# A tuned transformer block rewritten: Strassen in the Q, K and V projections, an accumulator begun from a PSUM copy, hand-mapped memory, and transposes by DMA

## The chip, the cores and the metric

One core of a Trainium2 chip. The metric is the device time of one execution in microseconds (us), median of several runs. The kernel before takes 828.0 us (four runs, 825.25 to 830.36). All comparisons are between runs of the fast state; one slow run occurred and is set apart below, and one run stands alone, so that its state is unknown (d_pin_again).

Names used here: PE is TensorE's matmul stream and PEld its weight loads, DVE is VectorE, ACT is ScalarE, POOL is GpSimd, SP is the engine whose queue issues the DMAs. L574 means line 574 of the kernel in question.

## The reference

One block: layer norm, linear attention with feature map phi, output projection, residual; then layer norm, a gated ReLU unit, down projection, residual. S = 2048 tokens, D = 1024, F = 3584, 32 heads of 32.

```python
def _A_ref(x, wqkv, wo):                      # cut
    q, k, v = qkv[0], qkv[1], qkv[2]
    phi = lambda t: jnp.where(t > 0, t + 1, jnp.exp(t)) + 1e-6
    pq, pk = phi(q), phi(k)
    kv = jnp.einsum("bhsd,bhse->bhde", pk, v)
    z = jnp.einsum("bhsd->bhd", pk)
    num = jnp.einsum("bhqd,bhde->bhqe", pq, kv)
    den = jnp.einsum("bhqd,bhd->bhq", pq, z)[..., None] + 1e-6
    o = num / den
    return (...)(o, 0, 2, 1, 3).reshape(B, S, D) @ wo

def _B_ref(x, W_gate, W_up, W_down):          # cut
    gate = jnp.einsum("bsd,df->bsf", x, W_gate)
    up = jnp.einsum("bsd,df->bsf", x, W_up)
    gate = gate * (lambda x, dt: x.astype(dt))(gate > 0, gate.dtype)
    return jnp.einsum("bsf,fd->bsd", gate * up, W_down)

h = x + _A_ref(_layernorm(x, axis=-1), A_wqkv, A_wo)
h2 = h + _B_ref(_layernorm(h, axis=-1), B_W_gate, B_W_up, B_W_down)
```

## The kernel before

One level of Strassen (seven products of half size instead of eight) is already used in gate/up and in the down projection, with the products ordered so that three accumulate in one PSUM bank. Q, K and V are plain products. All 384 transposes of 128x128 are TensorE matmuls against an identity, eight to a PSUM bank, copied out by ScalarE (half of the first tile's by VectorE). Memory comes from pools, so the down weights can be loaded only when the gate/up pools close.

The instruction order of each engine is fixed when the kernel is built: a scheduler places every instruction by when it believes it to be ready. An engine then runs its list in order.

```python
def kproj(t):                                   # plain products; V and Q likewise
    ...
        for kc in range(KC):
            nc.tensor.matmul(ps[:, :NW], lhsT=xnT[:, kc, t * P:(t + 1) * P],
                             rhs=wkv_sb[:, kc, j * NW:(j + 1) * NW], ...)
...
def oT():                                       # attention: transpose on TensorE
    pt = ps_tp()
    for c in range(KC):
        nc.tensor.transpose(pt[:, c, :], st["o"][:, c * P:(c + 1) * P], ident[:])
    st["oT"] = bwork.tile([P, KC, P], BF16, tag="oT", name="oT")
    nc.scalar.copy(out=st["oT"][:], in_=pt[:])
...
def part1():                                    # gate/up: C11 = M1 + M2
    st["A"] = A = ps2.tile([P, 2, SW], FP32, tag="d", name="A")
    prod(A, 1, True)
    m1 = snap(A, "m1")                          # ScalarE copies M1 to SBUF
    Dp = ps2.tile([P, 2, SW], FP32, tag="d", name="Dp")
    prod(Dp, 2, True)
    finish_sum(Dp, m1, 0)                       # VectorE adds
...
b = []                                          # down weights: after the pools close, for each half
for k, h in ((0, 0), (1, 0), (0, 1), (1, 1)):
    x = dpool.tile([P, FH, DW], BF16, tag="wd", bufs=5, name="wd")
    nc.sync.dma_start(out=x[:], in_=wd_v[:, k * FH:(k + 1) * FH, h * DW:(h + 1) * DW])
    b.append(x)
```

Of the kernel before, what the change touches and what calls it, by code (L numbers as in the profile page):

```python
# [29 lines left out]

@with_exitstack
def block_kernel(ctx: ExitStack, tc: tile.TileContext, x, wqkv, wo, wg, wu, wd, out, H: int):
# [7 lines left out]
    assert Dh == 32 and D % P == 0 and S % P == 0 and F % P == 0  # L40
    HPC = P // Dh
    ST = S // P
    KC = D // P
    FC = F // P
    TB = min(512, S)
    NTB = S // TB
    TPB = TB // P
    HB = min(256, TB)
    NHB = TB // HB
    NW = min(512, D)  # L50
    NKB = D // NW
    CPB = NW // P
    NDW = P + HPC
    GPB = 512 // NDW
    n_kv_banks = (KC + GPB - 1) // GPB
    assert TPB * H <= 512

    _load_act_set(nc)

    consts = ctx.enter_context(tc.tile_pool(name="consts", bufs=1))  # L60
    ident = consts.tile([P, P], BF16, name="ident")
    from concourse.masks import make_identity

    make_identity(nc, ident[:])
    mask = consts.tile([P, NDW], FP32, name="mask")
# [5 lines left out]
    psctx = ExitStack()  # L71
    pspool = psctx.enter_context(tc.tile_pool(name="ps", bufs=1, space=PSUM))
    _xy = [0]

    def ps_tp():
        return pspool.tile([P, KC, P], BF16, tag="tp", bufs=2, name="tp")

    def ps_x(nm="x"):
        return pspool.tile([P, 512], FP32, tag="x", bufs=2, name=nm)

    def ps_y(nm="y"):
        return pspool.tile([P, 512], FP32, tag="y", bufs=4, name=nm)

    def ps_xy(nm="xy"):
        _xy[0] += 1
        return ps_x(nm) if _xy[0] % 3 != 0 else ps_y(nm)

    pqctx = ExitStack()
    pq_pool = pqctx.enter_context(tc.tile_pool(name="pq", bufs=1, side="right"))
    pqT = pq_pool.tile([P, KC, S], BF16, name="pqT")  # L90
    kvz = pq_pool.tile([P, KC, NDW], BF16, name="kvz")
    wo_sb = pq_pool.tile([P, KC, D], BF16, name="wo_sb")

    def phi_from_psum(ps_ap, dst_ap, pool, width):
        e = pool.tile([P, width], FP32, tag="phi_e", name="phi_e")
        nc.scalar.activation(out=e[:], in_=ps_ap, func=ACT.Exp)  # L96
        e2 = pool.tile([P, width], FP32, tag="phi_e2", name="phi_e2")
        nc.vector.tensor_scalar(out=e2[:], in0=e[:], scalar1=1.0, scalar2=PHI_EPS,
                                op0=ALU.min, op1=ALU.add)
        nc.vector.scalar_tensor_tensor(out=dst_ap, in0=ps_ap, scalar=0.0, in1=e2[:],  # L100
                                       op0=ALU.max, op1=ALU.add)

    qctx = ExitStack()
    qpool = qctx.enter_context(tc.tile_pool(name="qpool", bufs=1))
    qwork = qctx.enter_context(tc.tile_pool(name="qwork", bufs=2))
    wq_sb = qpool.tile([P, KC, D], BF16, name="wq_sb")
    xnT = qpool.tile([P, KC, S], BF16, name="xnT")
    wqkv_v = wqkv.rearrange("(kc p) n -> p kc n", p=P)

    def q_proj(b, ps_fn):  # L110
        for c in range(KC):
            ps = ps_fn("qp")
            for kc in range(KC):
                nc.tensor.matmul(ps[:, :TB], lhsT=wq_sb[:, kc, c * P:(c + 1) * P],  # L114
                                 rhs=xnT[:, kc, b * TB:(b + 1) * TB],
                                 start=(kc == 0), stop=(kc == KC - 1))
            phi_from_psum(ps[:, :TB], pqT[:, c, b * TB:(b + 1) * TB], qwork, TB)

    NQA = min(2, NTB)

    with ExitStack() as actx:
        apool = actx.enter_context(tc.tile_pool(name="apool", bufs=1))
        xpool = actx.enter_context(tc.tile_pool(name="xpool", bufs=min(6, ST)))
        awork = actx.enter_context(tc.tile_pool(name="awork", bufs=2))
        asmall = actx.enter_context(tc.tile_pool(name="asmall", bufs=4))

        ps_mm = ps_xy
        wkv_sb = apool.tile([P, KC, 2 * D], BF16, name="wkv_sb")
        kv_ps = [ps_y("kv_ps") for _ in range(n_kv_banks)]

        x_tiles = {}

        def load_x(t):
            x_sb = xpool.tile([P, D], BF16, tag="x_sb", name="x_sb")
            nc.sync.dma_start(out=x_sb[:], in_=xf[t * P:(t + 1) * P, :])
            x_tiles[t] = x_sb

        load_x(0)
        nxt = 1
        for j in range(NKB):  # L140
            nc.sync.dma_start(out=wkv_sb[:, :, j * NW:(j + 1) * NW],
                              in_=wqkv_v[:, :, D + j * NW:D + (j + 1) * NW])
            if nxt < min(TPB, ST):
                load_x(nxt)
                nxt += 1
        while nxt < min(TPB, ST):
            load_x(nxt)
            nxt += 1
        for j in range(NKB, 2 * NKB):
            nc.sync.dma_start(out=wkv_sb[:, :, j * NW:(j + 1) * NW],  # L150
                              in_=wqkv_v[:, :, D + j * NW:D + (j + 1) * NW])
        while nxt < min(6, ST):
            load_x(nxt)
            nxt += 1
        for j in range(NKB):
            nc.sync.dma_start(out=wq_sb[:, :, j * NW:(j + 1) * NW], in_=wqkv_v[:, :, j * NW:(j + 1) * NW])
        nc.sync.dma_start(out=wo_sb[:], in_=wo.rearrange("(kc p) n -> p kc n", p=P))

        def ln_T(t):
            if t not in x_tiles:  # L160
                load_x(t)
            x_sb = x_tiles.pop(t)
            nsub = (D + 511) // 512
            fm = D // nsub
            stats = asmall.tile([P, nsub, nc.vector.BN_STATS_DIM], FP32, tag="stats", name="stats")
            for i in range(nsub):
                nc.vector.bn_stats(out=stats[:, i, :], in_=x_sb[:, i * fm:(i + 1) * fm])  # L167
            mv = asmall.tile([P, nc.vector.BN_AGGR_DIM], FP32, tag="mv", name="mv")
            nc.vector.bn_aggr(out=mv[:], in_=stats[:])
            lnv = asmall.tile([P, 1], FP32, tag="lnv", name="lnv")  # L170
            nc.scalar.activation(out=lnv[:], in_=mv[:, 1:2], func=ACT.Ln, bias=LN_EPS, scale=1.0)
            rstd = asmall.tile([P, 1], FP32, tag="rstd", name="rstd")
            nc.scalar.activation(out=rstd[:], in_=lnv[:], func=ACT.Exp, scale=-0.5)
            xn = awork.tile([P, D], BF16, tag="xn", name="xn")
            nc.vector.tensor_scalar(out=xn[:], in0=x_sb[:], scalar1=mv[:, 0:1], scalar2=rstd[:],  # L175
                                    op0=ALU.subtract, op1=ALU.mult)
            pt = ps_tp()
            for kc in range(KC):
                nc.tensor.transpose(pt[:, kc, :], xn[:, kc * P:(kc + 1) * P], ident[:])  # L179
                if t == 0 and KC >= 2 and kc == KC // 2 - 1:  # L180
                    nc.vector.tensor_copy(out=xnT[:, 0:KC // 2, t * P:(t + 1) * P], in_=pt[:, 0:KC // 2, :])
            if t == 0 and KC >= 2:
                nc.scalar.copy(out=xnT[:, KC // 2:KC, t * P:(t + 1) * P], in_=pt[:, KC // 2:KC, :])
            else:
                nc.scalar.copy(out=xnT[:, :, t * P:(t + 1) * P], in_=pt[:])

        def kproj(t):
            pk = awork.tile([P, D], BF16, tag="pk", bufs=TPB + 2, name="pk")
            for j in range(NKB):
                ps = ps_mm("kp")  # L190
                for kc in range(KC):
                    nc.tensor.matmul(ps[:, :NW], lhsT=xnT[:, kc, t * P:(t + 1) * P],  # L192
                                     rhs=wkv_sb[:, kc, j * NW:(j + 1) * NW],
                                     start=(kc == 0), stop=(kc == KC - 1))
                phi_from_psum(ps[:, :NW], pk[:, j * NW:(j + 1) * NW], awork, NW)
            return pk

        def vproj_kv(t, pk):
            v_sb = awork.tile([P, KC, NDW], BF16, tag="v_sb", name="v_sb")
            nc.gpsimd.memset(v_sb[:, :, P:NDW], 1.0)  # L200
            for jj in range(NKB):
                j = NKB + jj
                ps = ps_mm("vp")
                for kc in range(KC):
                    nc.tensor.matmul(ps[:, :NW], lhsT=xnT[:, kc, t * P:(t + 1) * P],  # L205
                                     rhs=wkv_sb[:, kc, j * NW:(j + 1) * NW],
                                     start=(kc == 0), stop=(kc == KC - 1))
# [10 lines left out]
        for g in range(NTB):  # L218
            pks = {}
            for tt in range(TPB):  # L220
                t = g * TPB + tt
                if t + 1 < ST:
                    ln_T(t + 1)
# [13 lines left out]
    for b in q_proj_rest:  # L237
        q_proj(b, ps_y)
# [383 lines left out]
```

## Time and profile before

| | before |
|---|---|
| time, median (range) | 828.0 us (825.25 to 830.36) |
| profiled span | 825.0 us |
| TensorE busy | 782.2 us, 95%, 4,016 matmuls |
| first projection matmul | 10.65 us |
| Q/K/V | to 196.5 us |
| attention and output projection | to 298.6 us |
| gate/up | to 641.6 us |
| wait for the down weights | 8.0 us |
| down projection | to the end |

Lines of the page of the kernel before: busy time per engine, the DMA engines' mean busy share in tenths over 40 slices, two matmul groups (after the bar: busy us, mean ns of one, then idle time before them and what ended it), and one group of DMA issues (size, median us to landing).

```profile
span 825.0 us, 10025 instructions
...
PE 782.2 (95%) x4016; PEld 369.1 (45%) x4016; DVE 506.7 (61%) x845; ACT 216.2 (26%) x337; POOL 3.6 (0%) x31
...
DMA  9700000530222200040401304040000983892001
...
L510 PE MATMUL accA<-wd,hh 128*128 128x512 f16 (+1 forms) x336 | 74.9, 385 | 8.0 <-DMA wd<-in_B_W_down_dram 8.0
L315 PE MATMUL attn<-wo_sb,oT 128*128 128x512 bf16 x256 | 61.2, 387 | 10.8 <-ACT oT L304 10.7
...
wd<-in_B_W_down_dram SPq DMA_DIRECT2D x8, 1792.0 KB, 9.7
```

Read it so: TensorE is busy 95% of the span, so it bounds the kernel; the hole is in the L510 line, 8.0 us in which TensorE sat idle until the down weights (wd) landed. The L315 line shows 10.7 us of waits for transposed attention tiles. In back-to-back stretches 56 matmuls of 128x512 take 12.09 us, 0.216 us each; the mean of about 380 ns that the page gives is the time from the start of one pipelined matmul to its end, which overlaps with the next, and not what it costs. The DMA digits of the attention stage (the tenth to the fifteenth of the 40) are 0 to 2: the DMA engines are nearly idle there.

Two windows of the attention stage of the kernel before; columns are stretch, length, then busy us and number of instructions per engine, the granted clock, the DMA engines' busy share and GB/s.

```profile
core 0: us, PE busy (x) PEld busy (x) DVE busy (x) ACT busy (x) POOL busy (x), PEclk, DMA share, GB/s
...
215.00:235.00 20.00, 18.03 (x137) 10.20 (x136) 18.87 (x52) 7.22 (x18) 0.00 (x0) 1.00 0.29 93
235.00:255.00 20.00, 17.37 (x149) 10.52 (x148) 18.73 (x56) 8.55 (x20) 0.00 (x0) 1.00 0.29 97
```

VectorE (third group, 18.87 and 18.73 of 20 us) is full here, TensorE is not.

### The profile page before, as it was taken

To read this page: it belongs to the slowest core of one execution; us is meant where nothing else is said; L and a number is where in the kernel's file an instruction comes from. 1 tells how busy PE (TensorE), PEld (TensorE's weight loads), DVE (VectorE), ACT (ScalarE), POOL (GpSimd) and SP (SyncE) were. 2 spreads that over 40 slices of the span, in tenths; PEclk is the share of its full clock that TensorE was granted. 3 is DMA by queue.
4 is the path that set the end of the run, shared out by engine and by line. 5 is a ranking of instruction groups with operands and counts; after the bars stand their busy time and mean duration, and the time that the engine had idled before them with its cause. 6 is when DMAs were issued, how large, how long until landed. Compare 5 with 4: busy or idle time off the path is not lost.

```text
span 825.0 us, 10025 instructions
## 1 busy us (share of the span) xinstructions
PE 782.2 (95%) x4016; PEld 369.1 (45%) x4016; DVE 506.7 (61%) x845; ACT 216.2 (26%) x337; POOL 3.6 (0%) x31
## 2 busy tenths in 40 slices
PE   5999999998897979999999999999999699999998
PEld 3445554443454534444444444444444244444443
DVE  5756314386999965567657556765754784329832
ACT  3435434332334333322323332333332000000000
POOL 0000000000000000000000000000000000000000
PEclk9999999999999989999999999999999899999999
DMA  9700000530222200040401304040000983892001
GB/s 323 250 14 26 1 1 1 152 92 0 97 83 79 89 25 14 20 127 27 122 26 56 84 20 128 25 122 27 20 19 20 300 267 120 273 340 97 26 33 45
DMA packets 75678, 74.04 MB, mean 90 GB/s; under 512 B 3440, under 2 KB 67952, under 8 KB 75120
## 3 DMA queue, kind: packets, MB, share of 16 engines
q1 hardware_dynamic: 75632, 73.41, 27.9%
q8 instruction: 31, 0.51, 0.3%
q14 instruction: 15, 0.12, 0.1%
HBM read 57.67 MB, written 15.73 MB: 89 GB/s over the span
## 4 chain that ended last, share of the span: by engine, by line
PE 59%; DVE 2%; DMA 2%; issue 1%; ACT 0%; SPq 0%; ACTq 0%
PE A L396 24%; PE E L396 12%; PE accA L510 10%; PE Dp L396 6%; PE accE L510 6%; PE accD L510 1%; DMA wd<-in_B_W_down_dram 1%; DMA hres<-h_dram_1898 1%; DVE s_6330 L534 0%; DVE hh L536 0%; DVE o L522 0%; DVE wd L548 0%; DVE s_6331 L535 0%; ACT u_5732 L410 0%; DVE hh_5749 L447 0%
## 5 line engine op out<-in xcount | busy, mean ns | idle before, releaser
L510 PEld LDWEIGHTS <-hh 128*128 128x128 bf16 (+1 forms) x560 | 55.1, 99 | 75.5 <-issue 10.6
L510 PE MATMUL accA<-wd,hh 128*128 128x512 f16 (+1 forms) x336 | 74.9, 385 | 8.0 <-DMA wd<-in_B_W_down_dram 8.0
L315 PE MATMUL attn<-wo_sb,oT 128*128 128x512 bf16 x256 | 61.2, 387 | 10.8 <-ACT oT L304 10.7
L396 PEld LDWEIGHTS <-tg 128*128 128x128 f16 x448 | 43.8, 98 | 54.2 <-issue 1.4
L396 PEld LDWEIGHTS <-tu 128*128 128x128 f16 x448 | 43.8, 98 | 52.9
L205 PE MATMUL vp<-wkv_sb,xnT 128*128 128x512 bf16 x256 | 59.8, 379 | 0.0
L192 PE MATMUL kp<-wkv_sb,xnT 128*128 128x512 bf16 x256 | 59.6, 388 | 0.0
L114 PE MATMUL qp<-xnT,wq_sb 128*128 128x512 bf16 x256 | 56.2, 379 | 1.3 <-DVE pqT L100 1.3
L396 PEld LDWEIGHTS <-wg 128*128 128x128 bf16 x336 | 33.2, 99 | 41.6 <-issue 2.9
L396 PEld LDWEIGHTS <-wu 128*128 128x128 bf16 x336 | 33.2, 99 | 40.9 <-issue 2.2
L315 PEld LDWEIGHTS <-oT 128*128 128x128 bf16 x256 | 23.6, 99 | 38.2 <-ACT oT L304 13.6
L114 PEld LDWEIGHTS <-wq_sb 128*128 128x128 bf16 x256 | 24.9, 98 | 30.9 <-issue 1.9
L192 PEld LDWEIGHTS <-xnT 128*128 128x128 bf16 x256 | 25.0, 100 | 28.0 <-issue 2.2
L205 PEld LDWEIGHTS <-xnT 128*128 128x128 bf16 x256 | 24.0, 97 | 24.6
L445 ACT ACTIVATE rg<-A 128x512 bf16<-128x512 f32 x28 | 16.7, 597 | 68.1 <-PE A L396 68.1
L304 ACT COPY oT<-tp 128x1024 bf16<-128x1024 bf16 x16 | 16.2, 1012 | 55.9 <-PE tp L302 55.9
L417 DVE SCALAR_TENSOR_TENSOR hh<-gu 128x512 bf16<-128x512 bf16 x42 | 29.0, 690 | 1.0
L96 ACT ACTIVATE phi_e<-qp 128x512 f32<-128x512 f32 x32 | 19.1, 597 | 39.1 <-PE qp L114 37.8
L175 DVE TENSOR_SCALAR xn<-x_sb,mv,rstd 128x1024 bf16<-128x1024 bf16 x16 | 8.7, 544 | 33.4 <-PE tp L179 31.1
L208 ACT CAST v_sb<-vp 128x512 bf16<-128x512 f32 x32 | 18.7, 585 | 39.8 <-PE vp L205 39.6
L167 DVE BATCH_NORM_STATS2 stats<-x_sb 128x6 f32<-128x512 bf16 x32 | 20.4, 671 | 9.8 <-DMA x_sb<-in_A_x_dram 9.8
L96 ACT ACTIVATE phi_e<-kp 128x512 f32<-128x512 f32 x32 | 19.1, 596 | 27.0 <-PE kp L192 27.0
(589 smaller groups left out, 1250.4 us busy)
## 6 DMA issues: line engine op xcount, KB each, us to landing
wd<-in_B_W_down_dram SPq DMA_DIRECT2D x8, 1792.0 KB, 9.7
wg<-in_B_W_gate_dram SPq DMA_DIRECT2D x14, 512.0 KB, 5.0
wu<-in_B_W_up_dram SPq DMA_DIRECT2D x14, 512.0 KB, 6.7
x_sb<-in_A_x_dram SPq DMA_DIRECT2D x16, 256.0 KB, 7.8
wkv_sb<-in_A_wqkv_dram SPq DMA_DIRECT2D x4, 1024.0 KB, 8.9
x_res<-in_A_x_dram SPq DMA_DIRECT2D x16, 256.0 KB, 2.8
out_dram<-o SPq DMA_DIRECT2D x32, 128.0 KB, 1.8
wq_sb<-in_A_wqkv_dram SPq DMA_DIRECT2D x2, 1024.0 KB, 11.0
```

The lines of the kernel that those rows point to most:

```text
L96: nc.scalar.activation(out=e[:], in_=ps_ap, func=ACT.Exp)
L114: nc.tensor.matmul(ps[:, :TB], lhsT=wq_sb[:, kc, c * P:(c + 1) * P], rhs=xnT[:, kc, b * TB:(b + 1) * TB], start=(kc == 0), stop=(kc == KC ...
L167: nc.vector.bn_stats(out=stats[:, i, :], in_=x_sb[:, i * fm:(i + 1) * fm])
L192: nc.tensor.matmul(ps[:, :NW], lhsT=xnT[:, kc, t * P:(t + 1) * P], rhs=wkv_sb[:, kc, j * NW:(j + 1) * NW], start=(kc == 0), stop=(kc == KC ...
L205: nc.tensor.matmul(ps[:, :NW], lhsT=xnT[:, kc, t * P:(t + 1) * P], rhs=wkv_sb[:, kc, j * NW:(j + 1) * NW], start=(kc == 0), stop=(kc == KC ...
L208: nc.scalar.copy(out=v_sb[:, jj * CPB:(jj + 1) * CPB, 0:P], in_=ps[:, :NW].rearrange("p (c e) -> p c e", e=P))
L304: nc.scalar.copy(out=st["oT"][:], in_=pt[:])
L315: nc.tensor.matmul(ps[:, :NW], lhsT=st["oT"][:, c, :], rhs=wo_sb[:, c, j * NW:(j + 1) * NW], start=(c == 0), stop=(c == KC - 1))
L396: nc.tensor.matmul(ps[:, x, :], lhsT=w[x][m - 1][:, kc, :], rhs=left[m - 1][:, kc, :], start=(start and kc == 0), stop=(kc == KH - 1), ski ...
L417: nc.vector.scalar_tensor_tensor(out=d, in0=gu[:, 0, :], scalar=0.0, in1=gu[:, 1, :], op0=ALU.max, op1=ALU.mult)
L445: nc.scalar.activation(out=rg[:], in_=A[:, 0, :], func=ACT.Relu)
L510: nc.tensor.matmul(acc[:], lhsT=lhs[:, f, tt * P:(tt + 1) * P], rhs=rhs[:, f, :], start=(start and f == 0), stop=(f == FH - 1), skip_group ...
```

## The change

Intent: fewer TensorE matmuls (Strassen in Q, K and V; transposes moved to DMA), less VectorE work in the attention stage, one VectorE addition less per gate/up quad (the second accumulator starts as a PSUM-to-PSUM copy of the first product), and memory laid out by hand so that the down weights can be loaded early. It is a rewrite; this is its core, with cuts.

```diff
+# one Strassen quad; A, D, E are PSUM banks
+    def p2(self):
+        D = self.ring()
+        self.fork(D, self.A)          # ScalarE copies M1, PSUM to PSUM
+        self.prod(D, 2, False)        # M2 accumulates on it
+        self.c11(D)
 ...
-            ps = ps_mm("kp")
-            for kc in range(KC):
-                nc.tensor.matmul(ps[:, :NW], lhsT=xnT[:, kc, t * P:(t + 1) * P], ...)
+        def prod(ps, m, start):       # K, V: pair p is the tiles p and p + 8
+            for kc in range(KH):
+                nc.tensor.matmul(ps, lhsT=left[m - 1][:, kc, :], rhs=right[m - 1][:, kc, :], ...)
 ...
-            for kc in range(KC):
-                nc.tensor.transpose(pt[:, kc, :], xn[:, kc * P:(kc + 1) * P], ident[:])
+            for k in range(2):
+                nc.sync.dma_start_transpose(out=XH[i][k][:, :, r:r + P], in_=xn[:, k * 512:(k + 1) * 512])
 ...
-            pt = ps_tp()
-            for c in range(KC):
-                nc.tensor.transpose(pt[:, c, :], st["o"][:, c * P:(c + 1) * P], ident[:])
+            nc.sync.dma_start_transpose(out=self.oT, in_=o)
 ...
+    for p in range(NP):               # K and V
+        pk, kq = k_quad(p)
+        qs.run(kq)
+        if p + 1 < NP:
+            ln_pair(p + 1)            # layer norm, normalisation on GpSimd, transpose by DMA
+        v, vq = v_quad(p)
+        qs.run(vq)
+        if p + 1 < NP:
+            x_sums(p + 1, 1)          # VectorE: Strassen operand sums of the next pair
 ...
+    hh1_ring = ring_of([at(132 + i, [SW]) for i in range(8)])     # spilled gate/up results
 ...
-            x = dpool.tile([P, FH, DW], BF16, tag="wd", bufs=5, name="wd")
+    wdb = [at(a, [FH, DW]) for a in (180, 128, 142, 156)]         # b11, b21, b12, b22; KB addresses
+    for x_, (k, h) in zip(wdb, ((0, 0), (1, 0), (0, 1), (1, 1))):
+        nc.sync.dma_start(out=x_, in_=wd_v[:, k * FH:(k + 1) * FH, h * DW:(h + 1) * DW])
```

## The prediction

> **What bounds the kernel now.** TensorE. The page gives it 95% busy of an 825 us span; VectorE 61%, ScalarE 26%. In the back-to-back stretches of the timeline 56 matmuls of 128x512 take 12.09 us, so one costs 0.216 us. By the windows and the timeline: first projection matmul at 10.7 us; Q/K/V to 196.5 us, TensorE full; attention and output projection 196.5 to 298.6 us; gate/up to 641.6 (28 quads of 12.09 = 338.5 of 343 us); 7.9 us in which TensorE waits for the down weights (the waits view: 8.0 us); down projection 175.5 us, of which 784 matmuls are 169.3. Only the attention stage is not TensorE-bound: VectorE is busy about 90% there, one 128-row tile every 5.65 us, about 107 us of VectorE work for 16 tiles, while TensorE's own work is about 78 us (256 large matmuls 55 us, 128 small and 256 transposes at about 0.06 us).
>
> **What the change does.**
> 1. Strassen in Q, K, V only (the output projection stays plain): 768 large matmuls become 672, 96 x 0.216 = -20.7 us.
> 2. 352 of the 384 TensorE transposes go to DMA: -21 us of TensorE work, all of it critical in the Q/K/V stage (-6), the rest in attention.
> 3. Attention VectorE work falls: BN_STATS (2 x 0.69), reciprocals and adds (1.07) and the 0.54 normalisation leave VectorE for ScalarE and GpSimd. By my sum 6.7 falls to about 3.9 us a tile, 62 us, below TensorE's 63. The second half of Q and the first gate/up products are interleaved there. I expect 78 us instead of 102, about 15 of them waits.
> 4. The down weights' memory is hand-mapped: the first block is loaded before gate/up ends (-8), and the weight combinations are not built twice for the second half (20 us of VectorE, mostly off the path; the stage falls by 2 to 3).
> 5. Added: PSUM-to-PSUM copies on ScalarE (1.01 us for 128x1024, as the snapshots). In gate/up the copy goes to a bank that the previous quad's last product leaves: its multiply (0.69) and the copy (1.01) must fit behind 9 matmuls (1.94 us). With about 0.1 us hand-overs that is even or 0.1 to 0.2 us short per quad: +3 to 6 us, offset by little.
> 6. Start: the first seven products need all four weight blocks and their VectorE sums (1.22 us each), for K and again for V. About 16 us of idle before steady state instead of 10.7: +5.
>
> DMA transposes of 128x1024 have no duration in this trace. The Trainium skill, "DMA: Bandwidth & Descriptors", Latency and other measured facts, gives 261 GB/s for DMA transpose; 256 KB is then an estimated 1 us, plus about 2 us as this trace's small transfers take. Two steps of lag (about 8 us) cover that.
>
> **Sum.** 16 + 161 (Q/K/V: 672 x 0.216 + 10 small + 6 waits) + 78 + 344 + 173 = 772; against a profile 3 us below the median.
>
> **Predicted: 770 us, 80% range 746 to 808. Faster by over 2%: 0.90, within 2%: 0.06, slower: 0.04.**
>
> **What would show it.** Page: TensorE near 96% busy; about 3,584 matmuls; VectorE under 460 us busy. Windows: gate/up 340 to 348 us; no 8 us hole before the down projection. Waits: TensorE waiting for the PSUM copy, under 0.3 us each. DMA issues: transposes landing in 2 to 4 us.
>
> **What would make it wrong.** Transposes that cost several us of DMA or queue time each: two per tile, in order on one queue with all loads; every engine runs a fixed order, so a late one stalls VectorE and then all. GpSimd normalisations over about 3 us, same result. The copy waiting for the whole product rather than half: 0.7 us per quad, +20 us.

## The result

| | before | after |
|---|---|---|
| time, median (range) | 828.0 us (825.25 to 830.36, 4 runs) | 791.55 us (788.05 to 793.07, 4 runs) |
| profiled span | 825.0 us | 790.3 us |
| TensorE busy | 782.2 us | 750.6 us, 3,583 matmuls |
| VectorE busy | 506.7 us | 459.2 us |

The ratio after to before is 0.9555 (95% interval 0.9525 to 0.9584). Ratios here are the mean time of one kernel's fast runs over the mean of the other's fast runs of the same rounds, so they are not quite the ratios of the medians that stand beside them.

The change is faster by 4.5%, about 22 us short of the point that was predicted. The page of the kernel after:

```profile
span 790.3 us, 9417 instructions
...
PE 750.6 (95%) x3583; PEld 341.0 (43%) x3583; DVE 459.2 (58%) x744; ACT 255.7 (32%) x481; POOL 41.2 (5%) x58
...
DMA  9355100318797833204022140310311920561011
...
L574 PE MATMUL psum<-mem 128*128 128x512 f16 (+1 forms) x1568 | 343.3, 379 | 1.2 <-ACT psum L270 1.1
...
L676 PE MATMUL psum<-mem 128*128 128x512 f16 (+1 forms) x784 | 172.1, 383 | 7.5 <-DVE mem L700 7.5
...
L321 PE MATMUL psum<-mem 128*128 128x512 f16 (+1 forms) x448 | 107.2, 394 | 13.6 <-DVE mem L343 5.0
```

TensorE is still 95% busy, with less to do. Gate/up (L574) waits 1.1 us in all for the PSUM copies (L270). The down group (L676) still has a hole, 7.5 us, but it now waits for VectorE (L700) and no longer for a DMA. The K/V group (L321) has 13.6 us of waits where the groups of K and V of before had none. And the DMA digits of the attention stage (tenth to fourteenth) are 7 to 9.

The same two windows of the attention stage, kernel after:

```profile
215.00:235.00 20.00, 16.88 (x84) 7.85 (x85) 16.41 (x44) 8.95 (x33) 3.62 (x3) 0.91 0.93 210
235.00:255.00 20.00, 18.27 (x106) 8.94 (x104) 12.34 (x32) 9.39 (x37) 6.16 (x4) 1.00 0.82 178
```

VectorE has room now (12.34 of 20 us in the second), but the DMA engines' share has gone from 0.29 to 0.93 and 0.82.

To see where TensorE's time goes I counted the matmuls of each stretch and took 0.2159 us for a large one and 0.062 us for a small one; what is left of the stretch is called lost. This is an estimate, good to about 1 us a row. It is given only for profiles with complete matmul records (as many matmuls as weight loads). The kernel after also runs 15 warm-up matmuls before its first product; they are not counted as work. Half clock counts as lost time, too. The last two columns are experiments that come below.

| lost TensorE time, us | before | after | operand sums pinned | one transpose per tile |
|---|---|---|---|---|
| start to 12 (before: to 10.65) | 9.4 | 10.8 | 10.4 | 10.1 |
| 12 to 100 | 2.4 | 18.9 | 11.4 | 8.2 |
| 100 to 200 | 4.7 | 1.7 | 2.7 | 2.4 |
| 200 to 300 | 20.9 | 16.0 | 14.0 | 15.9 |
| 300 to 608 (before: to 640) | 3.2 | 2.1 | | |
| from there to the end | 13.8 | 13.5 | | |

The sums: before loses 54.4 us and after 63.0, so TensorE's work fell by about 43 us (825.0 - 54.4 against 790.3 - 63.0). That is what 96 large matmuls (20.7 us) and 352 transposes (21.8 us at 0.062) come to. The expected saving of work is all there; 8.6 us of it net were given back as lost time: the Q/K/V stage (12 to 200 us) lost 13.5 us more than before, the attention stage 4.9 less. Some of the row from 12 to 100 is no wait: the granted clock was 0.50 from 12 to 16 us and 0.80 from 16 to 20 in this profile of the kernel after, 0.66 and 1.00 with operand sums pinned, and full with one transpose per tile. From 20 to 100 us alone the lost time is 14.9, 8.7 and 6.1 us in the three.

**The down hole.** TensorE's timeline of the kernel after around 608 us (start, length, group, in brackets the idle time just before it and what ended it):

```profile
start us, us, engine line op out<-in xcount [idle before <-releaser]
...
608.44 11.17 PE L676 MATMUL psum<-mem 128*128 128x512 bf16 x51
627.08 5.17 PE L676 MATMUL psum<-mem 128*128 128x512 f16 x12 [7.46 <-DVE mem L700]
```

Product 1 of the down projection (with five matmuls before 608) ends at 619.6. Then nothing for 7.46 us, and then 12 matmuls in 5.17 us, 0.43 us each, twice the usual. The built kernel, printed with a line of its own for each product, shows that six matmuls of product 6 stand ahead of product 2 in TensorE's list. Product 6 needs a chain of twelve VectorE subtractions of 2.02 us; product 2 needs a single weight block, b21. The queue that issues the loads, in the same stretch:

```profile
611.00 0.38 SPq L641 DMA_DIRECT2D mem<-in_B_W_down_dram  x1
613.50 0.32 SPq L582 DMA_DIRECT2D hh_dram<-mem  x1
613.91 5.71 SPq L641 DMA_DIRECT2D mem<-in_B_W_down_dram  x2
```

The first line is the load of b12; then the last spilled gate/up result (128 KB); then, in the third group, b22 at 613.9 and b21 only at 619.24. The view of waits of that queue:

```profile
engine line waited for: us in total, times, longest us
...
SPq L641 <- DMA hh_dram<-mem: 4.7, 1, 4.7
```

The issue of b21 waited 4.7 us for the spill to land, because the hand-made map gives b21 memory that the last spilled results still occupy.

**The Q/K/V stage.** VectorE's timeline of the kernel after near 95 us, then the TensorE group that was held:

```profile
start us, us, engine line op out<-in xcount [idle before <-releaser]
...
89.51 1.23 DVE L287 SCALAR_TENSOR_TENSOR mem<-mem 128x1024 bf16<-128x1024 f32 x1
94.48 0.43 DVE L248 TENSOR_TENSOR mem<-mem 128x512 f16<-128x512 bf16 x1 [3.75 <-DMA mem<-mem]
94.82 0.68 DVE L343 TENSOR_TENSOR mem<-psum,mem 128x512 bf16<-128x512 f32 x1
```

```profile
95.56 10.48 PE L321 MATMUL psum<-mem 128*128 128x512 bf16 x40 [2.00 <-DVE mem L343]
```

L248 is the first operand sum of the next pair; it waits 3.75 us for a transpose by DMA. Behind it in VectorE's list stands L343, an addition of the V result whose inputs were ready (the ScalarE copy that it needs ended at 91.18), and which frees the PSUM bank that TensorE needs. TensorE waits 2.00 us for it. This is how an engine with a fixed order passes one late transfer on to all. Some such waits were also followed by a lower clock:

```profile
core 0: us, PE busy (x) PEld busy (x) DVE busy (x) ACT busy (x) POOL busy (x), PEclk, DMA share, GB/s
44.00:48.00 4.00, 2.22 (x10) 0.74 (x8) 3.58 (x6) 1.26 (x3) 0.77 (x1) 1.00 0.74 162
48.00:52.00 4.00, 3.84 (x10) 1.39 (x11) 2.17 (x6) 0.58 (x1) 0.00 (x0) 0.57 0.60 152
...
626.00:630.00 4.00, 2.92 (x7) 0.99 (x8) 4.00 (x3) 0.00 (x0) 0.00 (x0) 0.50 1.11 379
```

The column before the DMA share is the granted clock. After the wait of 1.69 us that ended at 46.89 it was 0.57 from 48 to 52, and 0.50 from 626 to 630 after the wait of 7.46 us. The Trainium skill, "TensorE: Matmul & The Clock Gate", What's actually happening, states that the array drops to half rate after an idle window of about 3.4 us and needs as long a busy stretch to come back. The way back took 5.17 us here after the hole, somewhat more than one such window. That the clock fell after a wait of 1.69 us goes further than the page, but the length of a wait alone does not decide it: after waits of 1.34 us (ended at 64.62) and 1.65 us (at 70.74) it stayed full, and so it did in the trace of d_hh (below), whose Q/K/V stage is the same, after waits of 2.14 us (ended at 54.75) and 1.94 us (at 96.51). What decides stays open. So the same waits cost clock in one execution and none in another, and a part of each difference of a few us below can be this.

### The profile page after: what moved, and what is told of

Read it like the earlier page. It is cut to its first block, busy times and chain, and to the rows that moved or that the text cites. A ratio compares the mean times of both kernels' runs of the same rounds, so it can differ in the third digit from the quotient of the medians.

```text
span 790.3 us, 9417 instructions
## 1 busy us (share of the span) xinstructions
PE 750.6 (95%) x3583; PEld 341.0 (43%) x3583; DVE 459.2 (58%) x744; ACT 255.7 (32%) x481; POOL 41.2 (5%) x58
## 4 chain that ended last, share of the span: by engine, by line
PE 80%; DVE 6%; issue 5%; DMA 4%; ACT 2%; POOL 2%; SPq 1%; DVEq 0%; POOLq 0%; ACTq 0%
PE psum L574 41%; PE psum L676 20%; PE psum L321 7%; PE psum L418 6%; PE psum L482 4%; DMA mem<-mem 2%; DVE mem L700 2%; DMA mem<-in_A_wqkv_dram 1%; PE psum L458 1%; DVE mem L484 1%; POOL mem L240 1%; POOL mem L497 1%; DMA mem<-in_B_W_gate_dram 1%; ACT mem L274 1%; ACT mem L492 0%
## 5 line engine op out<-in xcount | busy, mean ns | idle before, releaser
L574 PE MATMUL psum<-mem 128*128 128x512 f16 (+1 forms) x1568 | 343.3, 379 | 1.2 <-ACT psum L270 1.1
L574 PEld LDWEIGHTS <-mem 128*128 128x128 f16 (+1 forms) x1568 | 152.8, 98 | 186.9 <-issue 7.6
L676 PE MATMUL psum<-mem 128*128 128x512 f16 (+1 forms) x784 | 172.1, 383 | 7.5 <-DVE mem L700 7.5
L602 DVE TENSOR_TENSOR mem<-psum,mem 128x1024 bf16<-128x1024 f32 x56 | 68.5, 1224 | 115.3 <-ACT mem L586 92.1
L676 PEld LDWEIGHTS <-mem 128*128 128x128 f16 (+1 forms) x784 | 77.1, 99 | 102.1 <-DVE mem L700 8.0
L321 PE MATMUL psum<-mem 128*128 128x512 f16 (+1 forms) x448 | 107.2, 394 | 13.6 <-DVE mem L343 5.0
L586 ACT COPY mem<-psum 128x1024 f32<-128x1024 f32 x56 | 56.7, 1012 | 111.8 <-PE psum L574 111.7
L321 PEld LDWEIGHTS <-mem 128*128 128x128 f16 (+1 forms) x448 | 44.5, 101 | 69.9 <-issue 19.8
L482 PE MATMUL psum<-mem 128*128 128x512 bf16 x256 | 60.1, 387 | 5.7 <-DMA mem<-mem 5.3
L592 ACT ACTIVATE mem<-psum 128x512 bf16<-128x512 f32 x56 | 33.4, 597 | 75.4 <-PE psum L574 75.4
L270 ACT COPY psum<-psum 128x1024 f32<-128x1024 f32 (+1 forms) x52 | 41.7, 803 | 37.1 <-DVE mem L594 29.8
L418 PE MATMUL psum<-mem 128*128 128x512 f16 (+1 forms) x224 | 52.6, 378 | 0.0
L700 DVE TENSOR_TENSOR mem<-mem 128x3584 f16<-128x3584 bf16 (+1 forms) x24 | 47.3, 2018 | 4.5 <-DMA mem<-hh_dram 2.7
L594 DVE TENSOR_TENSOR mem<-psum,mem 128x512 bf16<-128x512 f32 x56 | 38.7, 691 | 16.5 <-PE psum L574 12.6
L688 DVE TENSOR_TENSOR mem<-psum,mem 128x512 bf16<-128x512 f32 x32 | 22.1, 690 | 42.9 <-PE psum L676 42.7
L604 DVE SCALAR_TENSOR_TENSOR mem<-mem 128x512 bf16<-128x512 bf16 x56 | 38.7, 691 | 1.9
L418 PEld LDWEIGHTS <-mem 128*128 128x128 f16 (+1 forms) x224 | 21.2, 97 | 23.8 <-issue 2.2
```

The lines of the kernel that those rows point to most:

```text
L270: nc.scalar.copy(out=dst, in_=src)
L321: nc.tensor.matmul(ps, lhsT=left[m - 1][:, kc, :], rhs=right[m - 1][:, kc, :], start=(start and kc == 0), stop=(kc == KH - 1), skip_group_ ...
L418: nc.tensor.matmul(ps, lhsT=right[m - 1][:, kc, c * P:(c + 1) * P], rhs=left[m - 1][:, kc, :], start=(start and kc == 0), stop=(kc == KH - ...
L482: nc.tensor.matmul(ps, lhsT=self.oT[:, c, :], rhs=wo_sb[:, c, js], start=(c == 0), stop=(c == KC - 1))
L574: nc.tensor.matmul(ps[:, y, :], lhsT=w[y][m - 1][:, kc, :], rhs=left[m - 1][:, kc, :], start=(start and kc == 0), stop=(kc == KH - 1), ski ...
L586: nc.scalar.copy(out=u, in_=src)
```

## The experiments

My theory after reading the traces: (1) the down hole is a matter of order; (2) the Q/K/V waits come from late transposes together with VectorE's fixed order; (3) the PSUM copy costs nothing; (4) the transposes by DMA pay in the attention stage in spite of the load that they put on the DMA engines. Rivals: the data of product 2 are late themselves; VectorE simply has too much to do; the waits come from Strassen's sums and so cancel what Strassen saves in K and V.

| run | edit to the kernel after | median us | ratio to before |
|---|---|---|---|
| after | none | 791.55 | 0.9555 |
| d_pin | product 2 before product 6 | 795.05 | 0.960 (0.9577 to 0.9623) |
| d_pin_again | the same, one look | 792.1 | |
| d_hh | last spills off b21's memory | 780.05 | 0.9428 (0.9407 to 0.9449) |
| s_pin | operand sums behind V's addition | 783.63 | 0.9475 (0.9454 to 0.9497) |
| one_T | one transpose per tile in Q/K/V | 783.43 | 0.9464 (0.9442 to 0.9486) |
| kv_plain | K and V without Strassen | 794.23 | 0.9595 (0.957 to 0.9619) |
| gu_snap | no PSUM copy in gate/up | 792.58 | 0.9578 (0.9557 to 0.9599) |
| attn_peT | attention transposes on TensorE | 850.12 | 1.0272 (1.0243 to 1.0301) |
| att_peT2 | the same, a step later | 816.61 | 0.9867 (0.9838 to 0.9896) |
| att_lb | more lag and banks in attention | 789.64 | 0.9541 (0.952 to 0.9562) |
| best1 | s_pin + one_T + d_hh | 773.35 | 0.9347 (0.9322 to 0.9372) |
| best2 | best1 + two more | 771.0 | 0.9322 (0.9302 to 0.9341) |

All gave the right result. The runs came in rounds in which the kernel before had medians of 827.54, 826.92 and 827.04 us, against 828.0 in that of the kernel after. The ratios compare within a round, and by them the gains are somewhat smaller than by the medians, about 10.5 us for d_hh, 6.6 for s_pin and 7.5 for one_T. The intervals of d_pin, kv_plain, gu_snap and att_lb overlap with that of the kernel after, and that of best2 with that of best1: these differences are not clear of noise.

### d_pin and d_pin_again: product 2 first

```diff
-                nc.tensor.matmul(acc, lhsT=chunk(lhs, f)..., rhs=rhs[:, f, :], ...)
+                mm = nc.tensor.matmul(acc, lhsT=chunk(lhs, f)..., rhs=rhs[:, f, :], ...)
+                if pin and f == 0: tc.keep_in_program_order(mm)   # behind what was written before it
...
-            prod(A[tt], tt, sB, wd2, False)
+            prod(A[tt], tt, sB, wd2, False, pin=(s == 0))
```

> One edit to the changed kernel: in the first half of the down projection the first matmul of product 6 is pinned behind product 2 in TensorE's order (in the changed kernel six matmuls of product 6 stand ahead of product 2 and wait for VectorE's twelve subtractions until 627.1). Theory A (order): the hole of 7.5 us at 619.6 falls to under 1.5 us and the clock dip after it (about 2.6 us) goes with it, so 8 to 10 us come off 791.6: 781 to 784, ratio to before 0.943 to 0.947. Rival B (data): product 2's weights b21, whose load was issued at 611, are themselves late, so the hole only changes its owner to a DMA and the time stays within 2 us of 791.6. Rival C (VectorE): product 6 catches up with the subtractions later anyway, and the hole moves behind product 2: product 2 lasts 12.1 us, 619.6 to 631.7, longer than the 7.5 us that are missing, so no hole should appear there; if one does, it is under 1 us.

Measured: 795.05 us, no gain. Theory A failed. The first of its runs took 1122 us at a granted clock of 0.654 from end to end; it is not used for times. As the profile had fallen into that run, the kernel was run once more:

> The pinned kernel once more, for a profile in the fast state (the first profile of it fell in a slow run, clock 0.65). If b21's load, issued last at about 619 and landing about 10 us later, is what holds product 2 when product 2 goes first, the trace shows a wait of product 2 for a DMA of the down weights of 8.5 to 11 us ending at 628 to 631 in place of the 7.5 us wait for VectorE, and the time is 792 to 796. If instead there is no such wait, the reason for the pin's failure stays open.

Its TensorE timeline:

```profile
605.41 11.17 PE L676 MATMUL psum<-mem 128*128 128x512 bf16 x50
626.84 23.37 PE L676 MATMUL psum<-mem 128*128 128x512 bf16 x94 [10.26 <-DMA mem<-in_B_W_down_dram]
```

Product 2 now stands first and waits 10.26 us for a load of the down weights, in place of the 7.46 us for VectorE. The wait ended 1.2 us before the interval that I gave; its length and the time (792.1 us) were within theirs. Rival B was right: b21 is late itself. My text for d_pin had the cause of that wrong, though, for it took the load issued at 611 for b21; printing the four loads separately showed that b21 is issued last.

### d_hh: the memory that b21 waits for

```diff
+    hh1_last = ring_of([at(196 + i, [SW]) for i in range(8)])
...
-            return hh0(q, fc) if s == 0 else hh1_ring()
+            return hh0(q, fc) if s == 0 else (hh1_ring() if fc < FH - 2 else hh1_last())
```

> Reason for it: the pinned run was no faster, and its trace (slow state) shows product 2 waiting for a load of the down weights. The order of the queue in the changed kernel is b11 (560), b12 (611.0), b22 (613.9), and b21, which product 2 needs, last (619.24), because b21 shares memory with the last spilled gate/up results, and the last spill was issued at 613.5, behind the 1.8 MB of b12. One edit to the changed kernel: the results of the last two column blocks are put into 8 KB that are already free, so b21's memory is free earlier; the scheduler then issues b21 before the last spills and puts product 2 ahead of product 6 by itself (the build shows both). Theory A (memory reuse, then queue order, made the hole): the wait of 7.5 us and the half clock after it go, no new wait over 1 us in the down stage: 8 to 10 us less, 781 to 784, ratio 0.942 to 0.947. Rival B (VectorE's twelve subtractions until 627 limit whatever the order): product 6 waits instead, 789 to 792.

Measured: 780.05 us, 11.5 us less than the kernel after, slightly beyond the interval of theory A. The queue's timeline and TensorE's:

```profile
596.01 0.38 SPq L641 DMA_DIRECT2D mem<-in_B_W_down_dram  x1
...
608.80 0.38 SPq L641 DMA_DIRECT2D mem<-in_B_W_down_dram  x1
...
611.72 0.48 SPq L641 DMA_DIRECT2D mem<-in_B_W_down_dram  x1
```

```profile
606.24 34.05 PE L676 MATMUL psum<-mem 128*128 128x512 bf16 x155
```

b21 is issued at 596.0, before b12 (608.8) and b22 (611.7). From 606.24 on TensorE runs without a break (155 matmuls in 34 us in this cut of the timeline), and the view of waits shows none in the whole down stage. So the hole came from memory reuse: one 128 KB store in front of a load. (The hole and the half clock after it come to about 10 us. The rest is within the noise; in this profile the clock was also full after the waits of the Q/K/V stage, which the edit does not touch.) The store itself took 5.7 us to land against a median of 1.7 us for its kind, as it had been issued behind the 1.8 MB of b12. The Trainium skill, "DMA: Bandwidth & Descriptors", Queues, rings and completion order, says that on each DMA engine descriptors are consumed in ring order; this trace agrees with it. TensorE's odd order was the scheduler's answer to b21's late load: once the load is early, it puts product 2 first by itself.

### s_pin and one_T: the Q/K/V stage

s_pin changes VectorE's order and nothing else:

```diff
-        nc.vector.tensor_tensor(out=s1, in0=a21, in1=a22, op=ALU.add)
+        pin(nc.vector.tensor_tensor(out=s1, in0=a21, in1=a22, op=ALU.add))   # keep_in_program_order for pairs after the first
```

> One edit to the changed kernel: the first operand sum of each next pair in the Q/K/V stage (it waits for a transpose by DMA) is pinned behind the V addition traced before it on VectorE; no work is added or taken away. Theory A (VectorE's fixed order): the waits of K/V products for the V addition (1.69 us at 46.9, 1.34 at 64.6, 2.00 at 95.6) and the half clock after them go; lost TensorE time between 20 and 100 us falls from about 17 us to 6 to 10 us, total 782 to 787, ratio 0.945 to 0.951. Rival B (the transposes come too late anyhow): the wait moves to the next product, which needs the operand sums: K/V products wait for the sums instead, total within 2 us of 791.6. Rival C: amount of VectorE work in these 80 us, which the pin does not change: also within 2 us, with VectorE over 90% busy there.

Measured: 783.63 us. The place in VectorE's timeline that answers to the one shown above:

```profile
87.20 0.69 DVE L343 TENSOR_TENSOR mem<-psum,mem 128x512 bf16<-128x512 f32 x1 [0.48 <-ACT mem L274]
87.81 0.41 DVE L248 TENSOR_TENSOR mem<-mem 128x512 f16<-128x512 bf16 x1
```

L343 now runs first and L248 finds its transpose landed. Lost time from 12 to 100 us fell from 18.9 to 11.4 us. Not all of theory A came: the first of the three waits that it named is still there (1.65 us for L343, ended at 45.02), and the clock stayed full after it.

one_T leaves VectorE's order as it is and makes the transposes cheaper for the queue:

```diff
-            for k in range(2):
-                nc.sync.dma_start_transpose(out=XH[i][k][:, :, r:r + P], in_=xn[:, k * 512:(k + 1) * 512])
+            nc.sync.dma_start_transpose(out=at(16 * i, [KC, HS])[:, :, r:r + P], in_=xn)
```

> One edit to the changed kernel: in the Q/K/V stage each tile is transposed by one DMA of 128x1024 instead of two of 128x512. Theory A (the queue's issue time limits): issue time of the queue per tile falls from 3.2 us to about 1.9 us, the transposes land 1 to 4 us earlier, and waits at 70.7 and 95.6 that end with a transpose shrink: 786 to 790. Rival B (VectorE's order and the late statistics decide): the transposes wait for the normalised tile on GpSimd, not for the queue; total within 1.5 us of 791.6. If the issue time is in proportion to the columns and not per instruction, it stays 3.2 us a tile, which would also show here.

Measured: 783.43 us, better than theory A expected. The transposes of the Q/K/V stage, kernel after (24) and one_T (12): issue time in ns (min/median/max), first and last start, and time to landing.

```profile
L243 SPq DMA_TRANSPOSE mem<-mem x24: 1191/1244/1787, 38.7 to 91.9; - x24
...
DMA to landing us min/median/max: 2.4/2.5/3.7
```

```profile
L242 SPq DMA_TRANSPOSE mem<-mem x12: 1231/1232/2689, 36.3 to 81.6; - x12
...
DMA to landing us min/median/max: 3.0/3.2/4.0
```

The issue takes 1.24 us for 512 columns and 1.23 us for 1024: for these two widths it is a cost per instruction. In the kernel after GpSimd had the second tile of the pair ready at 89.05 us, but the last of the four transposes of the pair was issued at 91.9, behind the three others, and the sum that waited for it began at 94.48. With two per tile the second half lands about 1.24 + 2.5 us after the first issue begins, with one it is 3.2 us for all, and the queue is free for the next load 1.2 us earlier for each tile. What VectorE waited for transposes at L248 between 20 and 110 us, kernel after and one_T:

```profile
DVE mem L248 <- DMA mem<-mem: 7.1, 3, 3.7
```

```profile
DVE mem L248 <- DMA mem<-mem: 1.7, 2, 1.5
```

In s_pin this wait is absent. The order of L248, L343 and L295 in VectorE's list is the same in one_T as in the kernel after, so the same 7 us of waiting went in two ways: by transposes that come in time in the old order, or by an order in which nothing stands behind a late transpose. Neither the amount of VectorE work (rival C; both runs have the same within 1 us) nor the latency alone was the limit. The table of lost time puts 7.5 and 10.7 us into 12 to 100 us, of which 6.2 and 8.8 us lie between 20 and 100; the rest lies before 20 us, where the clock differs.

### kv_plain: what Strassen in K and V is worth

```diff
-        pk, kq = k_quad(p)
-        qs.run(kq)
+        pk = k_plain(p)          # four plain sums of 8 matmuls instead of seven products of 4
...
-        v, vq = v_quad(p)
-        qs.run(vq)
-        if p + 1 < NP:
-            x_sums(p + 1, 1)
+        v = v_plain(p)
+        x_sums(p, 1)             # now needed for Q alone
```

> One part of the change undone: K and V without Strassen (64 matmuls of 0.2159 us per pair and product instead of 56, 128 more in all... counted for K and V over 8 pairs: 64 against 56 for the two together, so 64 more, 13.8 us of TensorE work); operand sums are then needed for Q alone and nothing waits for them in this stage. Theory A (in the changed kernel the waits of this stage, 14.9 us between 20 and 100, ate the whole saving): those waits fall under 4 us, time 789 to 794. Rival B (the waits come from the transposes by DMA whatever the product): waits stay over 8 us, time 800 to 806.

Measured: 794.23 us, 2.7 us more than the kernel after, for 13.8 us more work. Neither theory holds whole. The waits did not go: they come to about 8 us between 38 and 75 us in its timeline (theory A said under 4). But the time is below rival B's interval. A part of the difference can be located: its start loses about 4 us less in the profile, as no product waits for sums of the weights and as the clock was full from 12 to 20 us in this profile (0.50 and 0.80 in that of the kernel after). VectorE's and TensorE's timelines show the same pattern as before:

```profile
72.11 0.43 DVE L248 TENSOR_TENSOR mem<-mem 128x512 f16<-128x512 bf16 x1 [6.18 <-DMA mem<-mem]
```

```profile
74.44 5.34 PE L352 MATMUL psum<-mem 128*128 128x512 bf16 x24 [2.27 <-DVE mem L363]
```

VectorE stands 6.18 us at L248 for a transpose, though no K or V product needs that sum any more, and TensorE waits 2.27 us for the K result (L363) queued behind it. So these waits come from a late transpose and the order, and not from a sum that a K or V product needs (the instruction that stands is still a Strassen sum, that of Q). It does not show that Strassen's sums cost nothing: about 11 us of the added work did not appear in the time, and only the start was located. In the kernel as it was changed, Strassen in K and V was worth about 3 us of its 13.8, which the noise does not tell from nothing. What it is worth once the waits are gone (in best1) was not run.

### gu_snap: the PSUM copy

```diff
-        self.fork(D, self.A)
-        self.prod(D, 2, False)
-        self.c11(D)
+        u1 = self.snap(self.A, 2)     # to SBUF, as before the change
+        self.prod(D, 2, True)
+        self.c11(D, u1)               # VectorE adds
```

> One edit to the changed kernel: in gate/up alone the accumulator is no longer begun from a PSUM copy; product 1 is copied to SBUF, product 2 starts its own sum and VectorE adds the two (as the kernel before did). Theory A (the PSUM copy costs TensorE nothing visible and saves VectorE work that is off the critical path there): time within 2 us of 791.6, gate/up still 12.1 us per 56 matmuls, VectorE's busy time higher by 20 to 50 us, over 459 us. Rival B (what the prediction said, 3 to 6 us lost on waits for the copy): time lower by 3 to 6 us, 786 to 789. Rival C (VectorE is nearly a limit in gate/up): time higher by over 3 us, with TensorE waiting for VectorE in gate/up.

Measured: 792.58 us, within the 2 us of theory A and not to be told from the kernel after. The busy line of its page:

```profile
PE 752.9 (95%) x3583; PEld 341.3 (43%) x3583; DVE 491.2 (62%) x772; ACT 237.3 (30%) x453; POOL 42.2 (5%) x58
```

VectorE works 491.2 us instead of 459.2, as expected, and nothing is gained or lost: VectorE is not what gate/up waits for. The copy of 128x1024 takes 1.00 us, and TensorE waited for such copies 1.1 us in all in gate/up.

### attn_peT and att_peT2: transposes of the attention stage back on TensorE

```diff
-            nc.sync.dma_start_transpose(out=self.oT, in_=o)
+            self.pe_T(self.oT, o)      # eight nc.tensor.transpose into one PSUM bank, one nc.scalar.copy; hn likewise
```

> One edit to the changed kernel: the 32 transposes by DMA in the attention stage become 256 TensorE transposes with one ScalarE copy each eight. Theory A (the transposes by DMA pay): 256 times about 0.062 us are 16 us more TensorE work, the 5.3 us of waits for the transposed tiles go: 7 to 13 us longer, 798 to 805. Rival B (the stage has 15 us of idle TensorE, in which they fit): within 3 us of 791.6. Theory C (DMA transposes are what delays the stage): shorter, 780 to 788.

Measured: 850.12 us, far above every expectation. The view of waits over the stage:

```profile
PE psum L503 <- DVE mem L465: 18.9, 13, 2.2
PE psum L458 <- DVE mem L484: 9.7, 15, 0.8
```

I had put each transpose right behind the VectorE work that feeds it (L465), in an engine that runs in order, and TensorE stood 18.9 us for it; the bank ring of three had two more users. The run showed a bad placement and not the price of the transposes. The second form has them one step later, as the kernel before had them, and eight banks:

```diff
-    LAGS = (0, 2, 4)               # nd, wo_h, sums
+    LAGS = (0, 1, 2, 3, 4)         # nd, transpose o, wo_h, transpose hn, sums
+    att = ring_of([5, 6, 7, 0, 1, 2, 3, 4])    # once Q is done
```

> A fairer form of the run with TensorE transposes in the attention stage, which had put them right behind the work that feeds them and so made TensorE wait 18.9 us for VectorE: here they come one step (one tile) after it, and the banks that Q leaves are used as well. Theory A (they fit if they are a step behind; the transposes by DMA save TensorE work but fill the DMA engines, 72 to 93% busy from 195 to 275 us against 11 to 29% in the kernel before): DMA share back to under 40%, TensorE work up by 16 us, lost time in the stage down from 15 to 4 to 10 us: 796 to 803. Rival B (any TensorE transpose must wait for its VectorE producer in this order): over 815.

Measured: 816.61 us, 25 us over the kernel after, and just over what rival B named. Two windows of it, to be held against those of the kernel after:

```profile
215.00:235.00 20.00, 14.59 (x80) 7.14 (x80) 15.39 (x41) 9.86 (x32) 2.40 (x2) 0.83 0.34 106
235.00:255.00 20.00, 16.36 (x109) 8.66 (x110) 10.32 (x26) 11.25 (x30) 3.65 (x3) 0.91 0.25 79
```

The edit also gives the tile before the transpose three buffers instead of two. The DMA share is back at 0.34 and 0.25. The waits of the stage still are about 16 us (5.9 of them for the ScalarE copies of the transposes, 3.3 for the GpSimd normalisation, 2.9 for L465), against 11 us in the kernel after; 16 us of TensorE work come on top, and the clock is lower (0.83 and 0.91 against 0.91 and 1.00). So the transposes by DMA are worth keeping against these two placements, though they fill the DMA engines. I did not try every placement; a better one on TensorE may exist.

### att_lb: more lag and more banks

```diff
-    LAGS = (0, 2, 4)
+    LAGS = (0, 3, 5)
-    oT_ring = ring_of([at(184 + 2 * i, [KC, P]) for i in range(2)])
+    oT_ring = ring_of([at(a, [KC, P]) for a in (184, 186, 136, 138)])
+    att = ring_of([5, 6, 7, 0, 1, 2, 3, 4])    # once Q is done
```

> Two settings of the attention stage of the changed kernel: the out projection follows three steps behind instead of two (four buffers for the transposed tile instead of two), and the five PSUM banks that the Q products leave are used by the last half of the stage. Same work. Theory A (latency and few buffers make the 15 us of lost TensorE time): the waits for transposed tiles (5.3 us) and for banks that VectorE frees (4.4 us) fall to under 3 us together: 783 to 787, ratio 0.945 to 0.951. Rival B (VectorE's amount of work, 86% busy from 195 to 215 and 82% to 235, is the limit): waits move to VectorE, 789 to 792.

Measured: 789.64 us; the intervals overlap with the kernel after. The waits for transposed tiles did fall (5.3 to 1.5 us), but others came: the view of waits of VectorE from 195 to 275 us has

```profile
DVE mem L484 <- DMA mem<-in_A_x_dram: 7.9, 4, 2.8
```

that is 7.9 us in which the residual addition waited for its x tile, loaded through the same queue and the same DMA engines, which are 93 to 95% busy from 215 to 255 us in this run. The wait moved to another transfer. Whether the order of the one queue or the full DMA engines made it late, this run does not separate. It was rival B in time, but not in cause: not VectorE's amount of work.

### best1 and best2

> The changed kernel with three edits at once: operand sums pinned behind the V addition, one transpose by DMA per tile in the Q/K/V stage, and the last gate/up results moved off b21's memory. The first two gave 8 us each alone (783.6 and 783.4). If both removed the same waits of the Q/K/V stage (lost time there was 14.9 us in the changed kernel, 8.7 and 6.1 in the two runs), they do not add: 10 to 12 us together, with 9 for the hole 770 to 773, ratio 0.930 to 0.934. If they are independent: 764 to 767.

Measured: 773.35 us, just over the upper edge of the first interval: s_pin and one_T remove the same waits and do not add (780.05 - 773.35 = 6.7 us for both, 8 us for each alone). best2 adds two edits:

```diff
-            xr = xr_ring()                                      # in wo_h
-            nc.sync.dma_start(out=xr, in_=xf[t * P:(t + 1) * P, :])
+            self.xr = xr_ring()                                 # in nd, two steps ahead; four buffers
+            nc.sync.dma_start(out=self.xr, in_=xf[self.t * P:(self.t + 1) * P, :])
...
-    WK.sums()
+    WK.sums(tc.keep_in_program_order)
```

> The three edits of the best run so far (773.35), and two more: the residual tile of the attention stage is loaded when its tile's step begins, two steps ahead, with four buffers (VectorE waited 7.7 us there in the changed kernel, and in the run with longer lags the trace names the residual's load for 1 to 2.8 us four times); and VectorE's first weight sum is pinned behind the first operand sums, so the copy of the first transposed tile does not stand behind a weight load. Theory A (late residual loads are one cause of the attention stage's waits): lost TensorE time there falls from 13 to 8 to 10 us, the start gains 1 us: 767 to 770. Rival B (the DMA engines are 80 to 93% busy with transposes there, so an earlier load delays a transpose): attention unchanged, 771 to 774.

Measured: 771.0 us, 2.35 us below best1, the fastest of all: 20.5 us below the kernel after. But the waits of the attention stage sum to 11.3 us (11.8 in best1), so the early residual load did nothing for their sum, as rival B said, though not for its reason: the waits for transposes fell (5.6 to 2.8 us) and a new one of 2.3 us for VectorE came. The intervals of best1 and best2 overlap; if there is a gain, the profiles put it into the start: the first K product begins its second group of matmuls at 10.87 us instead of 14.43. How much of that is the pin and how much the arrival of the second x tile, for which TensorE waited 0.8 us in best2 and 3.0 us in best1, one profile each does not settle. The clock goes with it: it was 0.50 from 12 to 16 us in the profile of best1 and full in that of best2, and the mean clock of the runs is 0.998 to 1.000 in best2, 0.991 to 0.998 in best1.

## Why the prediction was right or wrong

Predicted 770 us with a range of 746 to 808; measured 791.55. The direction and the range held, the point was about 22 us too low. The profile's span was predicted as 772 and was 790.3. Term by term:

- **Step 1 and 2, less TensorE work: right.** 3,583 matmuls for about 3,584, and the count of work fell by about 43 us for a predicted 42. The 32 transposes by DMA of the attention stage alone, put back on TensorE in the better of two placements, cost 25 us, of which 16 are work and the rest waits and clock of that placement.
- **The Q/K/V stage: the term that was mis-sized.** "161 (Q/K/V: 672 x 0.216 + 10 small + 6 waits)" allowed 6 us of waits. The profile has 18.9 us of lost time from 12 to 100 and 1.7 us from 100 to 200, some 14 us more (about 4 us of it lie before 20 us, with the half clock of the start). The mechanism stood in the last paragraph of the prediction ("every engine runs a fixed order, so a late one stalls VectorE and then all", "two per tile, in order on one queue"), as a danger, but I did not put it into the sum. s_pin and one_T showed it by taking about 8 us off each. What I had left out was the transpose's time on its queue: I estimated its landing from the 261 GB/s of the Trainium skill ("DMA: Bandwidth & Descriptors", Latency and other measured facts) and a latency. The landing came out as estimated (about 3 us; 3.2 us measured in one_T), but each instruction also took 1.24 us of issue time, for 512 columns as for 1024, so that the fourth transpose of a pair stood behind three others. And the "two steps of lag (about 8 us)" are those of the attention stage (`LAGS = (0, 2, 4)`); in the Q/K/V stage the program leaves one product, 28 matmuls or 6 us, between the layer norm of a pair and its sums.
- **Step 4, "the first block is loaded before gate/up ends (-8)": wrong.** The first block was loaded early (560 us) and the hole stayed, 7.46 us plus about 2.6 us at half clock (12 matmuls at 0.43 instead of 0.216): the down stage took 182 us for a predicted 173. The prediction looked at the first product and not at the second, whose weights shared memory with the last spills. d_hh, which moves 8 KB in each of the 128 partitions, took 11.5 us off, and with the hole gone the stage takes 171.8 us (606.24 to the end), so that the rest of the term was right.
- **Step 5, the PSUM copy "+3 to 6 us": wrong in size.** Gate/up ran at 12.09 us a quad with 1.1 us of waits, and gu_snap was no faster without the copy.
- **Step 3, the attention stage: right in size.** About 15 us of waits were predicted and 16.0 are lost from 200 to 300 us. Not foreseen was that the DMA engines would become 72 to 93% busy there. What the remaining waits come from is not settled: more lag (att_lb) and earlier residual loads (best2) only moved them.
- **Step 6, the start, "about 16 us": too high.** The first product began at 11.92 us.

In sum: start -4, Q/K/V waits +14, attention +1, gate/up -3, down +9 to +10: about +17 us of the 18 between 772 and 790. The errors that count are the two waits that were written down as "covered" and as "loaded before" the end of gate/up. That the range held in spite of them owes something to luck: the start and the PSUM copy had been put 7 us too high.

## What to carry to other kernels

When a slow engine's work is moved to a transfer, ask what stands behind the first consumer of that transfer in each engine's fixed list: pinning that one consumer behind work that is ready, or issuing one wide transfer instead of two, was worth about 8 us here, some 40% of what the 96 saved matmuls gave. When memory is mapped by hand, follow each late load back to the last user of its bytes, stores included, and check the second product as well as the first. Before work is taken off an engine, see whether the stage waits for that engine: 32 us of VectorE work less in gate/up bought nothing.

## What the Trainium skill lacked or had wrong

- "DMA: Bandwidth & Descriptors" gives the transpose a bandwidth, but an issue cost only in cycles, for "previous generations" and for other shapes, in a comparison with trn3. Here one transpose takes 1.23 to 1.24 us of the issuing queue for 128x512 as for 128x1024, and lands after 2.5 us (512 columns, median) or 3.2 to 3.5 us (1024).
- The same page's 261 GB/s could not be checked, as no run here has transposes alone. What it lacks is how much of the DMA engines they take: with two of 256 KB per tile the engines' share from 195 to 275 us is 0.72 to 0.93 at 150 to 210 GB/s of all kinds; without them it is 0.16 to 0.34.
- "VectorE: DVE Perf Modes", The three transpose paths, lists 390 ns for a 128x128 transpose on TensorE and 1309 ns by DMA. Back to back, eight TensorE transposes took 0.62 us here (0.08 each), and one transpose by DMA of eight such blocks lands in 3.2 us; the table's ratio (3.4) is that of single blocks, and for eight it was 5.2 here.
- "TensorE: Matmul & The Clock Gate", What's actually happening, puts the drop to half rate behind an idle window of about 3.4 us. Here waits of 1.69 and 2.00 us were followed by 4 us at 0.57 of full clock, waits of 1.34 and 1.65 us by none, and in d_hh waits of 2.14 and 1.94 us by none either. The page does not say what decides below one such window.
- No page that I found tells how a program on one core can run a whole execution at a clock of 0.654 (1122 us for 795, one run of all of these).
